# A layer of windowed attention and a gated MLP on one core: first-chunk norm in pairs, smaller first loads of Q and K, and crossbar-DMA transposes

## The chip, the core and the metric

The kernel runs on one core of one Trainium2 chip. The metric is device time in microseconds (us); lower is better. Times below are the median of 13 runs of the kernel before, and the profile is one execution taken with the hardware profiler.

## What is computed

One sequence of S = 2048 rows of width D = 640, in bf16. Both branches read the same normalised input, and everything is added to the residual:

```
xn  = layernorm(x)                                  # over D, no scale or shift
q, k, v = split(xn @ wqkv)                          # 32 heads of 20
scores  = (q @ k.T) * 20**-0.5, kept where 0 <= row - col < 256
attn    = softmax(scores) @ v @ wo
mlp     = (sigmoid(xn @ w_gate) * (xn @ w_up)) @ w_down     # F = 1536
out     = x + attn + mlp
```

## The kernel before

The rows are worked off in four chunks of 512 rows (`NCH`), each of four blocks of 128 rows (`SBC`). Heads go in eight groups of four (`NG`, `HG`): four heads lie in the four 32-row strips of TensorE, so that four small matmuls run side by side.

**Norm and turning.** `ln_block` (L191) takes the statistics of one block on VectorE and the power -1/2 on GpSimd. `norm_block` (L203) writes the normalised block `xn` on VectorE. The projections need it with D on the partitions, so `transpose_block` (L209) turns it with five TensorE transposes of 128 by 128 into PSUM, and ScalarE (chunk 0) or VectorE (chunks 1 to 3) copies it into `xnT`. `xnT` has two buffers (`xtp`), `xn` four.

**Q, K and V.** `proj_block` (L227) makes one of five column blocks of Q or K (five matmuls of 128x512), copies it to `st`, and SyncE's queue writes it to a scratch in DRAM (`sq`, `sk`). `spread` (L244) reads it back with each head in a strip of 32 partitions: `qT` and `kT`. The rows that pad 20 to 32 are zeroed once per scratch by `clear` (L147). `proj_v` (L251) makes V of one block in ten matmuls of 128x320.

**Attention.** A group in a chunk goes in steps of up to 512 columns (`STEPS`, L41: key block, first query block, number of query blocks). A step is one call of `scores` (L388): eight or four matmuls into `ps` (L394), two exponentials on ScalarE into `pT` (L400), and causal and window masks on GpSimd (L405, L409). `pv` (L413) multiplies a group's `pT` by V into `acc` (L420), and `finish_group` (L428) divides and turns the result on VectorE into `oc`. `pT` has four buffers. In chunk 0 there are no earlier keys, so its three steps per group are 384, 256 and 512 columns wide.

**MLP and output.** `g_gu` (L315) makes one of twelve column blocks of gate (L319, tanh at L322) and up (L326), joined on VectorE at L330 into `h`. `down` and `outp` (L342, L352) sum the MLP's second product and the attention's projection in one PSUM tile, add x and write out.

**What sets the order.** The order of instructions on every engine is the order of the program (`manual_schedule`). The scores' steps are the skeleton. Between steps, `Fill` (L443) issues dense TensorE work from a list of generators, in amounts that share what is left evenly over the columns that are left (L540); chunk 0's columns count 0.9. The list (L505 to L519) is gate and up of chunk 0 with norms and transposes of chunk 1 mixed in, Q and K of chunk 1 with the norms of chunk 2, V of chunk 1, one block of gate and up of chunk 1, the output of chunk 0 with the transposes of chunk 2, and so on. Three blocks of gate and up are issued ahead of the first scores (L525).

**SyncE's queue** issues nearly all DMAs, in order; a DMA that must wait for its data holds all later ones. Its order at the start is x of chunk 0 and the weights of V, Q, K, the first half of gate and up (L155), and the two clears; then the writes of `sq` and `sk` as they are made, with the whole of `qT` behind the second write of `sk` (L294), then `kT` of group 0 and of groups 1 to 7 (L298, L299); then `load_rest` (L159): the other half of gate and up, x of chunk 1, two clears, `wd`, four copies of `A_wo` into `wo_i`, four loads of `wo` that wait for those copies, and x of chunk 2. DMAs take turns on eight completion semaphores, so that a DMA also waits for the eighth before it.

The line that decides how much work stands between two steps is

```python
        credit += fill.left() * share(c, width) / weight
        weight -= share(c, width)
        credit = fill.pull(credit)
```

Of the kernel before, what the change touches and what calls it, by code (L numbers as in the profile page):

```python
# [8 lines left out]
P = 128  # L9
# [8 lines left out]
NCH = S // CW  # L18
# [26 lines left out]
)  # L45


def steps_of(c):
    out = []
    for pieces in STEPS:  # L50
        here = [p for p in pieces if c > 0 or p[0] >= 0]
        placed, col = [], 0
        for r, q0, n in here:
            placed.append((r, q0, n, col))
            col += n
        out.append((placed, col))
    return out
# [13 lines left out]
def kernel(  # L71
# [16 lines left out]
    def pool(name, bufs, **kw):  # L88
        return ctx.enter_context(tc.tile_pool(name=name, bufs=bufs, **kw))
# [6 lines left out]
    qp = pool("qp", 2)  # L96
    kp = pool("kp", 3)
    vp = pool("vp", 10)
    hp = pool("hp", 13)
    pp = pool("pp", 4)  # L100
    op = pool("op", 8)
    onp = pool("onp", 3)
    tp = pool("tp", 2)
    np_ = pool("np", 1)
    yp = pool("yp", 2)
# [45 lines left out]
    def load_gu(k):  # L151
        for t, w in ((wg, B_w_gate), (wu, B_w_up)):
            nc.sync.dma_start(out=t[k], in_=w.rearrange("(c p) f -> p c f", p=P)[:, :, k * FS:(k + 1) * FS])

    load_gu(0)  # L155
    clear("q", 0)
    clear("k", 0)

    def load_rest():  # L159
        for k in range(1, F // FS):  # L160
            load_gu(k)
        load_x(1)
        clear("q", 1)
        clear("k", 1)
        nc.sync.dma_start(out=wd, in_=B_w_down.rearrange("(c p) d -> p c d", p=P))
        wo_i = tc.dram_tile([HG, NG * DH, D], BF16, name="wo_i")
        for i in range(HG):
            nc.sync.dma_start(out=wo_i[i].rearrange("(g d) n -> g d n", d=DH),
                              in_=A_wo.rearrange("(g i d) n -> i g d n", i=HG, d=DH)[i])
        for i in range(HG):  # L170
            nc.sync.dma_start(out=wo[32 * i:32 * i + 32, :, :],
                              in_=wo_i[i].rearrange("(m j) n -> j m n", j=32))
        load_x(2)
# [17 lines left out]
    def ln_block(c, s):  # L191
        xs = xc[c][:, s, :]
        stats = lnp.tile([P, 2, nc.vector.BN_STATS_DIM], FP32, name="stats")
        for a in range(2):
            nc.vector.bn_stats(out=stats[:, a, :], in_=xs[:, a * 320:(a + 1) * 320])  # L195
        mv = lnp.tile([P, nc.vector.BN_AGGR_DIM], FP32, name="mv")
        nc.vector.bn_aggr(out=mv, in_=stats)
        rstd = lnp.tile([P, 1], FP32, name="rstd")
        nc.gpsimd.tensor_scalar(out=rstd, in0=mv[:, 1:2], scalar1=EPS, scalar2=None, op0=ADD)
        nc.gpsimd.tensor_tensor(out=rstd, in0=rstd, in1=neghalf, op=POW)  # L200
        return mv, rstd

    def norm_block(c, s, mv, rstd):  # L203
        xn = lnp.tile([P, D], BF16, name="xn", bufs=4)
# [1 line left out]
                                scalar2=rstd[:, 0:1], op0=SUB, op1=MULT)  # L206
        xns[c, s] = xn

    def transpose_block(c, s, act):  # L209
        xn = xns.pop((c, s))  # L210
        pt = ps_d.tile([P, DC, P], BF16, name="pt", tag="d")
        for d in range(DC):
            nc.tensor.transpose(pt[:, d, :], xn[:, d * P:(d + 1) * P], ident)  # L213
        dst = xnT[c][:, :, s * P:(s + 1) * P]
        if act:
            nc.scalar.copy(out=dst, in_=pt)
        else:
            nc.vector.tensor_copy(out=dst, in_=pt)

    def new_xnT(c):  # L220
        xnT[c] = xtp.tile([P, DC, CW], BF16, name="xnT")
# [44 lines left out]

    MM = 216

    def g_norms(c):

        new_xnT(c)
        stat = {}
        for s in range(SBC + 2):
            if s < SBC:
                stat[s] = ln_block(c, s)
                yield 0
            if s >= 2:
                norm_block(c, s - 2, *stat[s - 2])
                yield 0

    def g_transposes(c):
        for s in range(SBC):
            transpose_block(c, s, False)
            yield 5 * 64

    def chain(*gens):
        for g in gens:
            yield from g

    def g_qk(c):  # L290
        for w in "qk":
            for m in range(DC):
                proj_block(w, c, m)
                if w == "k" and m == 1:  # L294
                    spread("q", c, 0, NG)
                yield 5 * MM
        if c == 0:
            spread("k", c, 0, 1)  # L298
            spread("k", c, 1, NG)  # L299

    def g_v(c):
        for s in range(SBC):
# [82 lines left out]
            yield from outp(c, s, ys)  # L385


    def scores(c, g, placed, width):  # L388
        pt = pp.tile([P, HG, CW], BF16, name="pT")
        pss = [ps_s.tile([P, 2, CW], FP32, name="ps", tag="s") for _ in range(2)]  # L390
        for r, q0, n, col in placed:
            kc, kb = divmod(c * SBC + r, SBC)
            for i in range(HG):
                nc.tensor.matmul(  # L394
                    pss[i // 2][:, i % 2, col * P:(col + n) * P],
                    lhsT=qk["k", kc][32 * i:32 * i + DH, g, kb * P:(kb + 1) * P],
                    rhs=qk["q", c][32 * i:32 * i + DH, g, q0 * P:(q0 + n) * P],
                    start=True, stop=True)
        for a in range(2):
            nc.scalar.activation(out=pt[:, 2 * a:2 * a + 2, 0:width * P],  # L400
                                 in_=pss[a][:, :, 0:width * P], func=EXP, scale=SCALE)
        for r, q0, n, col in placed:
            if r >= 0:
                v = pt[:, :, col * P:(col + 1) * P]
                nc.gpsimd.affine_select(out=v, in_=v, pattern=[[0, HG], [1, P]], compare_op=GE,  # L405
                                        fill=0.0, base=0, channel_multiplier=-1)
            if q0 + n - 1 == r + 2:
                v = pt[:, :, (col + n - 1) * P:(col + n) * P]
                nc.gpsimd.affine_select(out=v, in_=v, pattern=[[0, HG], [-1, P]], compare_op=GE,  # L409
                                        fill=0.0, base=-1, channel_multiplier=1)  # L410
        return pt

    def pv(c, g, parts):  # L413
        acc = ps_a.tile([P, CW], FP32, name="acc")
        flat = [(pt, *piece) for placed, pt in parts for piece in placed]
        for k, (pt, r, q0, n, col) in enumerate(flat):
            v = vt[c * SBC + r]
            for i in range(HG):
                h = g * HG + i
                nc.tensor.matmul(  # L420
                    acc[32 * i:32 * i + 32, q0 * P:(q0 + n) * P],
                    lhsT=v[:, h * VW:h * VW + 32], rhs=pt[:, i, col * P:(col + n) * P],
                    start=(k == 0), stop=(k == len(flat) - 1), skip_group_check=True)
        finish_group(c, g, acc)
# [57 lines left out]
            yield cost  # L482

    new_xnT(0)
    stat = {0: ln_block(0, 0)}
    for s in range(SBC + 1):
        if s + 1 < SBC:
            stat[s + 1] = ln_block(0, s + 1)
        if s < SBC:
            norm_block(0, s, *stat[s])  # L490
            transpose_block(0, s, True)
        if s:
            proj_v(0, s - 1)
    for _ in g_qk(0):
        pass
    load_rest()
# [4 lines left out]
    def later(c):  # L501
        load_x(c)
        yield 0

    fill.add("gu0", mix(g_gu(0, 0, 12), chain(g_norms(1), g_transposes(1)), 9), 12 * GU + 1280)  # L505
    fill.add("qk1", mix(g_qk(1), g_norms(2), 2), 50 * MM)
    fill.add("v1", g_v(1), 40 * 136)
    fill.add("gu1a", g_gu(1, 0, 1), 1 * GU)
    fill.add("out0", mix(g_out(0), g_transposes(2), 1, 3), OUT + 1280)
    fill.add("x3", later(3), 0)  # L510
    fill.add("qk2", g_qk(2), 50 * MM)
    fill.add("v2", g_v(2), 40 * 136)
    fill.add("gu1b", mix(g_gu(1, 1, 12), g_norms(3), 10), 11 * GU)
    fill.add("out1", mix(g_out(1), g_transposes(3), 1, 3), OUT + 1280)
    fill.add("qk3", g_qk(3), 50 * MM)
    fill.add("v3", g_v(3), 40 * 136)
    fill.add("gu2", g_gu(2, 0, 12), 12 * GU)
    fill.add("out2", g_out(2), OUT)
    fill.add("gu3", g_gu(3, 0, 12), 12 * GU)  # L519

    todo = [(c, g, k, placed, width) for c in range(NCH) for g in range(NG)
            for k, (placed, width) in enumerate(steps_of(c))]
    share = lambda c, w: w * (0.9 if c == 0 else 1.0)
    weight = sum(share(c, w) for c, *_, w in todo)
    fill.pull(6 * 5 * MM)  # L525
    parts = {}
    credit = 0
    fill.shut = {"out0", "out1", "out2"}
    for t, (c, g, k, placed, width) in enumerate(todo):
        if g == 0 and k == 0 and c > 0:  # L530
            fill.until(f"qk{c}")
        if g == 0 and k == 2 and c > 0:
            fill.until(f"v{c}")
        if k == 1 and t > 3:
            before = todo[t - 3][0:2]
            pv(*before, parts.pop(before))
            if before[1] == NG - 1:
                fill.shut.discard(f"out{before[0]}")
        parts.setdefault((c, g), []).append((placed, scores(c, g, placed, width)))
        credit += fill.left() * share(c, width) / weight  # L540
        weight -= share(c, width)
        credit = fill.pull(credit)
    fill.pull(10 ** 9)

# [47 lines left out]
```

## Time and profile before

| | |
|---|---|
| median of 13 runs | 335.68 us (334.32 to 339.35) |
| the profiled execution: its own time, its span | 339.18 us, 337.5 us |
| TensorE busy (share of the span) | 319.7 us (95%) |
| ScalarE, GpSimd, VectorE busy | 218.4, 165.4, 163.4 us |
| mean granted TensorE clock | 0.99 |
| moved by DMA | 30.89 MB, mean 92 GB/s |

The profiled execution lies near the upper end of the 13 runs, 3.5 us above their median. Its time is 1.7 us more than its span. In the views, times are microseconds from the span's start. A row of the timeline gives start, length, engine, line, operation, tiles, count, and in brackets the idle time of the engine before it with what ended it. A row of the waits gives the total, the number and the longest. Matmuls are pipelined, so the distance between the starts of two rows tells more of what a matmul costs than its length: five matmuls of 128x512 start 1.08 us before whatever follows them. The row of 40 slices cuts the span into pieces of 8.4 us.

### The profile page before, as it was taken

Reading aid. Unit: us, or ns where it says so; the run is one execution under the profiler, and the core shown is the slowest. Engines: PE = TensorE matmul, PEld = TensorE weight load, DVE = VectorE, ACT = ScalarE, POOL = GpSimd, SP = SyncE. Lnnn points to the kernel's source line nnn. Section 1 sums busy time; section 2 is a strip of 40 time slices with the busy share of each in tenths; the row PEclk is TensorE's granted clock in tenths of the full one; section 3 lists DMA queues with packets and bytes.
Section 4 is the critical chain, followed back from the end, with each engine's and each line's share of the span. In section 5 each row is a group of like instructions: output and inputs, shape, how many; then the busy total and the mean of one; then the engine's idle time right before and its main releaser. Section 6 shows DMA issues by size and latency. Waiting matters only on the chain.

```text
span 337.5 us, 7190 instructions
## 1 busy us (share of the span) xinstructions
PE 319.7 (95%) x2855; PEld 166.3 (49%) x2884; DVE 163.4 (48%) x333; ACT 218.4 (65%) x274; POOL 165.4 (49%) x312
## 2 busy tenths in 40 slices
PE   5999878998999999999999999999999999999996
PEld 2654323444556654544445664544445665444664
DVE  4241239678763344655873436354443424444142
ACT  2424674877775667787875666878787666888300
POOL 5200239468665554664865555545555455554300
PEclk9699999999999999999999999999999999999999
DMA  7937798402720024530000002540000010000001
GB/s 260 378 121 217 252 383 286 119 33 82 213 81 22 19 64 163 175 126 0 3 2 19 21 21 94 183 150 2 2 0 3 21 40 20 2 0 2 0 13 66
DMA packets 26224, 30.89 MB, mean 92 GB/s; under 512 B 1456, under 2 KB 25648, under 8 KB 26160
## 3 DMA queue, kind: packets, MB, share of 16 engines
q1 hardware_dynamic: 25904, 30.20, 27.3%
q8 instruction: 22, 0.36, 0.4%
q10 hardware_dynamic: 288, 0.25, 0.2%
q14 instruction: 10, 0.08, 0.1%
HBM read 21.00 MB, written 10.26 MB: 93 GB/s over the span
## 4 chain that ended last, share of the span: by engine, by line
PE 82%; DMA 7%; ACT 4%; DVE 3%; issue 2%; POOL 1%; SPq 1%; POOLq 0%; ACTq 0%
PE y L345 15%; PE pqk L234 13%; PE pg L319 12%; PE pu L326 12%; PE ps L394 8%; PE pv L260 7%; PE y L358 7%; PE acc L420 6%; DMA xc<-in_A_x_dram 5%; ACT pT L400 3%; PE pt L213 1%; DMA sk<-st 1%; DVE stats L195 1%; POOL pT L405 1%; DVE t L430 0%
## 5 line engine op out<-in xcount | busy, mean ns | idle before, releaser
L400 ACT ACTIVATE pT<-ps 128x1024 bf16<-128x1024 f32 (+2 forms) x192 | 175.9, 971 | 61.8 <-PE ps L394 58.0
L405 POOL TENSOR_SCALAR_AFFINE_SELECT pT<-pT 128x512 bf16<-128x512 bf16 x128 | 82.1, 641 | 82.5 <-ACT pT L400 82.3
L409 POOL TENSOR_SCALAR_AFFINE_SELECT pT<-pT 128x512 bf16<-128x512 bf16 x112 | 72.1, 644 | 57.9 <-ACT pT L400 57.9
L330 DVE SCALAR_TENSOR_TENSOR h<-th,pu 128x512 bf16<-128x512 f32 x48 | 32.8, 682 | 60.0 <-PE pu L326 21.4
L319 PE MATMUL pg<-xnT,wg 128*128 128x512 bf16 x229 | 59.2, 380 | 2.6 <-DVE h L330 2.0
L326 PE MATMUL pu<-xnT,wu 128*128 128x512 bf16 x230 | 57.8, 380 | 1.2 <-issue 1.1
L345 PE MATMUL y<-wd,h 128*128 128x320 bf16 x384 | 57.3, 300 | 0.0
L234 PE MATMUL pqk<-xnT,wqkv 128*128 128x512 bf16 x192 | 45.8, 381 | 0.5 <-issue 0.2
L394 PE MATMUL ps<-qT,kT 20*128 20x384 bf16 (+2 forms) x704 | 39.6, 275 | 5.4 <-ACT pT L400 4.0
L345 PEld LDWEIGHTS <-h 128*128 128x128 bf16 x384 | 35.7, 98 | 16.8 <-issue 4.0
L322 ACT ACTIVATE th<-pg 128x512 f32<-128x512 f32 x48 | 28.8, 600 | 14.9 <-PE pg L319 14.8
L430 DVE STREAM_TRANSPOSE t<-acc 128x512 f32<-128x512 f32 x32 | 22.8, 713 | 28.5 <-PE acc L420 28.1
L319 PEld LDWEIGHTS <-wg 128*128 128x128 bf16 x240 | 22.1, 98 | 29.2 <-issue 5.5
L326 PEld LDWEIGHTS <-wu 128*128 128x128 bf16 x240 | 21.3, 98 | 27.0 <-issue 5.2
L234 PEld LDWEIGHTS <-wqkv 128*128 128x128 bf16 x200 | 22.3, 119 | 19.3 <-issue 2.9
L363 DVE SCALAR_TENSOR_TENSOR y_sb<-y,xc 128x320 bf16<-128x320 f32 x32 | 15.4, 490 | 32.6 <-PE y L358 32.6
L394 PEld LDWEIGHTS <-kT 20*128 20x128 bf16 x704 | 12.3, 92 | 37.0 <-issue 35.3
L260 PE MATMUL pv<-wqkv,xnT 128*128 128x320 bf16 x160 | 26.4, 319 | 0.3 <-DVE v L264 0.3
L420 PE MATMUL acc<-pT,v 128*32 128x384 bf16 (+2 forms) x704 | 25.7, 277 | 0.5 <-POOL pT L405 0.2
L358 PE MATMUL y<-wo,oc 128*128 128x320 bf16 x160 | 24.1, 299 | 0.0
L420 PEld LDWEIGHTS <-v 128*32 128x32 bf16 x704 | 15.0, 96 | 13.6 <-issue 11.0
L238 DVE CAST st<-pqk 128x512 bf16<-128x512 f32 x20 | 13.7, 687 | 15.4 <-PE pqk L234 13.7
(32 smaller groups left out, 176.8 us busy)
## 6 DMA issues: line engine op xcount, KB each, us to landing
qT<-sq SPq DMA_DIRECT2D x4, 1024.0 KB, 6.1
kT<-sk SPq DMA_DIRECT2D x3, 1024.0 KB, 5.5
sq<-st SPq DMA_DIRECT2D x20, 128.0 KB, 2.1
sk<-st SPq DMA_DIRECT2D x20, 128.0 KB, 3.3
wqkv<-in_A_wqkv_dram SPq DMA_DIRECT2D x3, 800.0 KB, 6.6
out_dram<-y_sb SPq DMA_DIRECT2D x15, 160.0 KB, 1.8
wg<-in_B_w_gate_dram SPq DMA_DIRECT2D x2, 960.0 KB
wu<-in_B_w_up_dram SPq DMA_DIRECT2D x2, 960.0 KB
```

The costliest lines, as they stand in the source:

```text
L234: nc.tensor.matmul(ps, lhsT=wt[:, m, :], rhs=xnT[c][:, d, :], start=(d == 0), stop=(d == DC - 1))
L260: nc.tensor.matmul(ps[:, 0:HALF], lhsT=xnT[c][:, d, s * P:(s + 1) * P], rhs=wqkv[:, d, 2 * D + hf * HALF:2 * D + (hf + 1) * HALF], start=( ...
L319: nc.tensor.matmul(pg, lhsT=part(wg, d, f), rhs=xnT[c][:, d, :], start=(d == 0), stop=(d == DC - 1))
L326: nc.tensor.matmul(pu, lhsT=part(wu, d, f), rhs=xnT[c][:, d, :], start=(d == 0), stop=(d == DC - 1))
L330: nc.vector.scalar_tensor_tensor(out=h, in0=th, scalar=1.0, in1=pu, op0=ADD, op1=MULT)
L345: nc.tensor.matmul(ys[hf], lhsT=ht[c, f][:, s * P:(s + 1) * P], rhs=wd[:, f, hf * HALF:(hf + 1) * HALF], start=(f == 0), stop=False)
L358: nc.tensor.matmul(ys[hf], lhsT=oc[c, m][:, s * P:(s + 1) * P], rhs=wo[:, m, hf * HALF:(hf + 1) * HALF], start=False, stop=(m == DC - 1))
L394: nc.tensor.matmul(pss[i // 2][:, i % 2, col * P:(col + n) * P], lhsT=qk["k", kc][32 * i:32 * i + DH, g, kb * P:(kb + 1) * P], rhs=qk["q", ...
L400: nc.scalar.activation(out=pt[:, 2 * a:2 * a + 2, 0:width * P], in_=pss[a][:, :, 0:width * P], func=EXP, scale=SCALE)
L405: nc.gpsimd.affine_select(out=v, in_=v, pattern=[[0, HG], [1, P]], compare_op=GE, fill=0.0, base=0, channel_multiplier=-1)
L409: nc.gpsimd.affine_select(out=v, in_=v, pattern=[[0, HG], [-1, P]], compare_op=GE, fill=0.0, base=-1, channel_multiplier=1)
L420: nc.tensor.matmul(acc[32 * i:32 * i + 32, q0 * P:(q0 + n) * P], lhsT=v[:, h * VW:h * VW + 32], rhs=pt[:, i, col * P:(col + n) * P], start ...
```

## The change

In words:

1. **Start.** The four blocks of chunk 0 are normed and turned in two pairs: statistics of two blocks, norm and transpose of both, then V of both. Before, each block's statistics came one block ahead of its norm, and V one block behind.
2. **First scores.** `qT` of groups 0 and 1 is loaded behind the second write of `sk`, then `kT` of group 0, `kT` of groups 1 and 2, the rest of `qT` and the rest of `kT`. x of chunk 1 is loaded ahead of the first clears instead of in `load_rest`.
3. **Steps of chunk 0.** Two groups share five steps of 512, 384, 512, 512 and 384 columns, where each group had three steps; 20 steps in place of 24. A group's `pv` comes ahead of the second step after its last one. Chunk 0's columns count fully in the sharing of fill.
4. **Turning.** For chunks 1 to 3 a DMA on SyncE's queue with `transpose=True` goes from `xn` to `xnT` in place of five TensorE transposes and a VectorE copy, 12 blocks in all. For chunks 1 and 2 each is issued soon behind its norm; for chunk 3, whose buffer is then still read, within the output of chunk 1. In chunks 1 to 3 the GpSimd half of the norm is issued one block later.
5. **Buffers and fill.** `h` 13 to 15, `oc` 8 to 7, `on` 3 to 2 buffers; three blocks of gate and up of chunk 1 ahead of the output of chunk 0 in place of one.

The diff, cut:

```diff
+STEPS0 = (
+    ((0, 0, 0, 3), (0, 3, 3, 1)),
+    ((0, 1, 1, 3),),
+    ((0, 2, 2, 2), (1, 2, 2, 2)),
+    ((1, 0, 0, 3), (1, 3, 3, 1)),
+    ((1, 1, 1, 3),),
+)
...
-    hp = pool("hp", 13)
+    hp = pool("hp", 15)
...
-    op = pool("op", 8)
-    onp = pool("onp", 3)
+    op = pool("op", 7)
+    onp = pool("onp", 2)
...
     load_gu(0)
+    load_x(1)
     clear("q", 0)
     clear("k", 0)
...
-        load_x(1)
...
+    def rstd_block(mv):
         rstd = lnp.tile([P, 1], FP32, name="rstd")
...
+    def turn_block(c, s):
+        nc.sync.dma_start(out=xnT[c][:, :, s * P:(s + 1) * P], in_=xns.pop((c, s)), transpose=True)
...
-    def g_norms(c):
+    def g_norms(c, turn):
...
+        mv, rstd = {}, {}
+        for k in range(SBC + 3):
+            if k < SBC:
+                mv[k] = ln_block(c, k)
+            if 0 <= k - 1 < SBC:
+                rstd[k - 1] = rstd_block(mv[k - 1])
+            if k < SBC:
                 yield 0
+            if 0 <= k - 2 < SBC:
+                norm_block(c, k - 2, mv[k - 2], rstd[k - 2])
                 yield 0
+            if turn and 0 <= k - 3 < SBC:
+                turn_block(c, k - 3)
+
+    def g_turns(c):
         for s in range(SBC):
-            transpose_block(c, s, False)
-            yield 5 * 64
+            turn_block(c, s)
+            yield 0
...
                 if w == "k" and m == 1:
-                    spread("q", c, 0, NG)
+                    spread("q", c, 0, NG if c else 2)
...
             spread("k", c, 0, 1)
-            spread("k", c, 1, NG)
+            spread("k", c, 1, 3)
+            spread("q", c, 2, NG)
+            spread("k", c, 3, NG)
...
-    stat = {0: ln_block(0, 0)}
-    for s in range(SBC + 1):
-        if s + 1 < SBC:
-            stat[s + 1] = ln_block(0, s + 1)
-        if s < SBC:
-            norm_block(0, s, *stat[s])
-            transpose_block(0, s, True)
-        if s:
-            proj_v(0, s - 1)
+    for s0 in range(0, SBC, 2):
+        mv = [ln_block(0, s) for s in (s0, s0 + 1)]
+        for s in (s0, s0 + 1):
+            norm_block(0, s, mv[s - s0], rstd_block(mv[s - s0]))
+            transpose_block(0, s)
+        for s in (s0, s0 + 1):
+            proj_v(0, s)
...
-    fill.add("gu0", mix(g_gu(0, 0, 12), chain(g_norms(1), g_transposes(1)), 9), 12 * GU + 1280)
-    fill.add("qk1", mix(g_qk(1), g_norms(2), 2), 50 * MM)
+    fill.add("gu0", mix(g_gu(0, 0, 12), g_norms(1, True), 9), 12 * GU)
+    fill.add("qk1", mix(g_qk(1), g_norms(2, True), 2), 50 * MM)
     fill.add("v1", g_v(1), 40 * 136)
-    fill.add("gu1a", g_gu(1, 0, 1), 1 * GU)
-    fill.add("out0", mix(g_out(0), g_transposes(2), 1, 3), OUT + 1280)
+    fill.add("gu1a", g_gu(1, 0, 3), 3 * GU)
+    fill.add("out0", g_out(0), OUT)
...
-    fill.add("gu1b", mix(g_gu(1, 1, 12), g_norms(3), 10), 11 * GU)
-    fill.add("out1", mix(g_out(1), g_transposes(3), 1, 3), OUT + 1280)
+    fill.add("gu1b", mix(g_gu(1, 3, 12), g_norms(3, False), 8), 9 * GU)
+    fill.add("out1", mix(g_out(1), g_turns(3), 1, 3), OUT)
...
-        if k == 1 and t > 3:
-            before = todo[t - 3][0:2]
-            pv(*before, parts.pop(before))
-            if before[1] == NG - 1:
-                fill.shut.discard(f"out{before[0]}")
+        for group in [x for x in ends if ends[x] == t - 2]:
+            pv(*group, parts.pop(group))
+            if group[1] == NG - 1:
+                fill.shut.discard(f"out{group[0]}")
...
-        credit += fill.left() * share(c, width) / weight
-        weight -= share(c, width)
+        credit += fill.left() * width / weight
+        weight -= width
```

In the changed program SyncE's queue holds the four turning DMAs of chunk 1 behind `load_rest`, that is behind the loads of `wo` and of x of chunk 2; those of chunk 2 stand among the last writes of `sk` of chunk 1, three of the four directly ahead of the load of that chunk's `kT`. Ten steps of scores and three `pv` come ahead of the first matmul of Q of chunk 1.

## The prediction on record

> **What bounds the kernel now.** I read the page first, then the chain of work that ended last, then the timeline of TensorE and of SyncE's queue in the first 75 us.
>
> ```profile
> PE 319.7 (95%) x2855; PEld 166.3 (49%) x2884; DVE 163.4 (48%) x333; ACT 218.4 (65%) x274; POOL 165.4 (49%) x312
> PE   5999878998999999999999999999999999999996
> ACT  2424674877775667787875666878787666888300
> PEclk9699999999999999999999999999999999999999
> DMA  7937798402720024530000002540000010000001
> PE 82%; DMA 7%; ACT 4%; DVE 3%; issue 2%; POOL 1%; SPq 1%; POOLq 0%; ACTq 0%
> ```
>
> TensorE is the bound: from the eleventh slice on (84 us) it is never under 0.9, so there only removed TensorE work can help. Before that, the slices with 8 and 7 hold waits, and the DMA row is high in the fifth to seventh (34 to 59 us: 7, 9, 8). In the chain, 7% is DMA.
>
> ```profile
> 36.57 0.34 PE L394 MATMUL ps<-qT,kT 20*128 20x384 bf16 x4 [0.98 <-DMA kT<-sk]
> ...
> 50.94 1.24 PE L319 MATMUL pg<-xnT,wg 128*128 128x512 bf16 x5 [1.32 <-DVE h L330]
> ...
> 54.33 1.24 PE L319 MATMUL pg<-xnT,wg 128*128 128x512 bf16 x5 [0.69 <-DVE h L330]
> ...
> 58.65 0.45 PE L213 MATMUL pt<-ident,xn 128*128 128x128 bf16 x5
> 58.94 1.24 PE L319 MATMUL pg<-xnT,wg 128*128 128x512 bf16 x5
> ```
>
> The first scores wait 0.98 us for `kT`. The two waits on VectorE have one root: VectorE's statistics of chunk 1 stand ahead of `h` and wait for x, 9.0 us in all:
>
> ```profile
> DVE stats L195 <- DMA xc<-in_A_x_dram: 9.0, 3, 5.3
> ```
>
> The last two timeline rows price a turning: five transposes start 0.29 us before what follows. SyncE's queue shows why x is late, and what a DMA put behind `load_rest` will meet:
>
> ```profile
> 27.28 0.41 SPq L249 DMA_DIRECT2D qT<-sq  x1
> 27.74 2.55 SPq L242 DMA_DIRECT2D sk<-st  x3
> 34.44 0.82 SPq L249 DMA_DIRECT2D kT<-sk  x2
> ...
> 36.47 1.65 SPq L118 DMA_DIRECT2D xc<-in_A_x_dram  x1
> ...
> 55.22 3.53 SPq L171 DMA_DIRECT2D wo<-wo_i  x4
> 58.80 0.65 SPq L118 DMA_DIRECT2D xc<-in_A_x_dram  x1
> ```
>
> The last `sk` writes share the DMA engines with 1 MB of `qT`; x of chunk 1, asked for at 36.47, lands 11.7 us later; the `wo` loads hold the queue until 58.75.
>
> **What the Trainium skill says.** "TensorE: Matmul & The Clock Gate", Part 1: the clock is granted by windows of 3.4 us, half speed after an idle one, full after a busy one. The trace agrees: the granted clock is 0.53 of full in 8 to 10 us and 0.76 in 14 to 16 (stage table), and ten V matmuls take 2.6 us there against 1.36 later. "DMA: Bandwidth & Descriptors", HWDGE ordering: each DMA engine consumes one queue's descriptors in order; it fits x landing late behind 3 MB. For the crossbar there are two prices far apart, and no row of before shows one. "Latency and other measured facts" of the same page: 261 GB/s. "VectorE: DVE Perf Modes", The three transpose paths: 1309 ns for 128x128.
>
> **The change, part by part,** against the profiled execution (339.2 us, span 337.5).
>
> *Start, -1.8.* Before, the second transpose waits for `xn` behind statistics of block 2, whose x landed at 7.51; V starts at 9.52. In pairs, `xn` of block 1 needs only `rstd` (GpSimd done at 7.06), so both transposes are out by 7.8, and the copy of block 0 by 7.6. V of two blocks starts at 7.8, half clock from 8.06. One full window later (11.5) the clock can be full: 13.5 of the 20 matmuls at 0.267 us, the rest at 0.136, end at 12.4; turning of blocks 2 and 3 with ScalarE's copy behind the V copies, to 13.7; 20 V matmuls, to 16.4. Q starts at 16.4 in place of 18.2. Bounds: -0.5 (no window gained) to -3.5 (never half).
>
> *First loads, -1.0.* With 256 KB of `qT` in place of 1 MB, the last `sk` write should land in 2.1 us (the median of `sq` writes) and not in 4.6. It is issued at 28.0, `kT` of group 0 at 30.4, 4.0 earlier than 34.44; landed at 32.4. Three blocks of gate and up end at 16.4 + 10.8 + 6.5 = 33.7, so `kT` is covered by them by 1.3 us and the 0.98 wait goes. Scores start at 33.7 (before 36.57).
>
> *x of chunk 1 early, -2.0* (1.32 + 0.69; bounds 0 and -2.4, from the distances of starts). Its 640 KB go to the end of the first DMA stretch, which is quiet from 18 us on, and delay the clears by 1.8 us; the first `sq` write comes about then. I cost that at nothing: 10 us of Q and K work cover it.
>
> *Transposes off TensorE, -3.4.* 12 blocks x 0.285. All stand in stretches where TensorE is full, or on its way to the next `xnT`. VectorE's 12 copies (0.49 each) go too, worth nothing by themselves.
>
> *Steps of chunk 0, -0.9.* Scores advance 0.33 (512 columns), 0.28 (384), 0.22 (256): eight groups x 0.83 = 6.6, four pairs x 1.55 = 6.2, so -0.4. A change between scores and dense work costs about 0.13 (ten Q matmuls start 2.29 before the next scores, 71.59 to 73.88, for 10 x 0.216); four fewer, -0.5.
>
> *Waits on exponentials in chunk 0, -1.5* (0 to -4). Idle rows <- ACT between 44 and 98 us sum to about 3.3. A step had 1.57 us of fill against 1.63 of exponentials (39.0 / 24) plus 0.44 of tanh; now 2.01 against 1.88 plus 0.56, so TensorE leads by more. I take under half.
>
> Sum: -10.6.
>
> *Second half of gate and up, +0.3* (0 to 1). It is due for the seventh block at about 42 to 43 us; 2.8 MB from 30.4 at the 370 GB/s of this stretch land at 39 to 43.
>
> *The turning DMAs of chunk 1, +3.0* (0 to 26). This is the new wait. Nothing is queued for TensorE but Q of chunk 1, which needs all four blocks. Need: 33.7 + ten scores (3.1) + three `pv` (1.8) + nine blocks (19.4) + changes (1.3) + waits left (1.3) = 60.6. Offer: the queue from `kT` on carries as many bytes as before (7.2 against 7.1 MB, x removed, Q and K split), so it shifts by the 4.0 us of `kT`: x of chunk 2 is issued at 54.8, and since DMA falls quiet at 63.4 before, landed near 59.5. The turning is behind it. 164 KB at 261 GB/s are 0.63 us; the other price gives 5 x 1.309 = 6.5. I take 0.75 per block and 1 us to land, near the first, as five turnings in one DMA share its start: 59.5 + 3 + 1 = 63.5, 2.9 late. SyncE's time to issue them (unknown, 0.4 as a plain DMA to 2) hides behind x if under 1.5.
>
> *Half clock after that wait, +0.6* (0 to 1.7): a 3 us gap may fill most of a window.
>
> *Chunks 2 and 3, 0.* Turning of chunk 2 is due after the output of chunk 0, some 30 us later; chunk 3's after that of chunk 1. Chunk 2's DMAs do stand ahead of `kT` of chunk 1, which before was issued at 89.99 and landed 0.3 us ahead of its scores; the extra work ahead of those scores (two more blocks of gate and up, 4.3 us) is the cover, and is gone if a block costs over 1.5. Buffers of `h`, `oc`, `on`: no wait is moved, as by the fill list's costs the output of a chunk ends some three steps before they are due.
>
> Net -10.6 + 3.9 = -6.7: 332.5 for an execution like the profiled one. That one lies 3.5 above the median of the 13 runs; part of the spread may be the half clock at the start, of which there is then less to gain, so I take -6.2 from the median: **329.5**.
>
> **Rivals.**
> *No wait for the turning.* If x of chunk 2 lands sooner or TensorE is later at Q of chunk 1: -10.3, so 325.9. For it: before, TensorE took 33.5 us from the first scores to Q of chunk 1 for some 28.7 of work counted the same way; a loss like that would cover it. Against: the queue's order.
> *Covers worth less.* Exponential waits stay, the start gains 0.5, x early 1.0, the turning waits 4: 333.5. For it: chunk 0's ScalarE row has 7s and 8s.
> *Slower: a slow crossbar.* At 6.5 us a block the turning of chunk 1 lands at 86.5: 26 us of wait and 1.7 of half clock, against -10.3: 353. It decides from about 2 us a block (4 x 2.05 + 1 + 59.5 is 8 us late, with the half clock all of the gain), and `kT` of chunk 1 adds to it. For it: the price of 1309 ns; before moved no data through the crossbar.
>
> **How the numbers follow.** Likeliest 0.45 (329.5, own range 326.5 to 332.5); no wait 0.23; covers worth less 0.15; slow crossbar 0.17. The low end takes in a start gain of 3.5; the high end, part of the slow crossbar: 323 to 340, leaving out some 4% below and 14% above. This kernel's measurement can tell about 0.5% (1.7 us) from no change. Faster: 0.45 + 0.23 + half of 0.15 = 0.75; same 0.08; slower 0.17.
>
> **What would show it.** Start: Q at 16.4. First loads: `kT` issued near 30.4, no wait before the first scores near 33.7. x: no VectorE wait for x of chunk 1. Turning: TensorE idle about 3 us ahead of the first Q of chunk 1, near 60 to 64, ended by a DMA; blocks landing 0.6 to 1 us apart. After chunk 0 no new idle. The forecast is wrong if the turning lands 2 us apart or more, if SyncE takes over 1.5 us to issue one, or if the queue reaches the turning at another time than 55.

## The result and the profile after

The changed kernel takes 331.99 us (median of 11 runs, 331.78 to 333.17); the kernel before, over the 48 runs that now lie beside it, takes 335.4 (334.19 to 339.35). The ratio is 0.9892, 95% interval 0.9863 to 0.992. The profiled execution of after took 331.86 us with a span of 330.1; that of before took 339.18 with 337.5. So the profiles differ by 7.4 us of span and the medians by only 3.4. That gap is the first thing to explain.

The rows of the page of after that answer to those of before (one digit is 8.25 us):

```profile
PE 313.8 (95%) x2795; PEld 161.0 (49%) x2824; DVE 159.7 (48%) x321; ACT 216.8 (66%) x266; POOL 166.0 (50%) x312
...
PE   6999979798999999999999999999999999999996
...
PEclk9999999999999999999999999999999999999999
DMA  7976999319700123640013113620000000000001
...
PE 75%; ACT 6%; DMA 6%; POOL 4%; DVE 4%; issue 2%; SPq 2%; ACTq 0%
```

TensorE is busy 5.9 us less (part of it is the half clock of before, which counts as busy; either trace lacks 29 matmul records), and its clock has no 6 in the second slice any more. But there are three slices below 9 in the middle (7, 7, 8 at 41, 58 and 74 us), and the chain still has 6% of DMA. TensorE's timeline names the three (brackets: idle time before the row, and what ended it):

```profile
14.68 10.96 PE L250 MATMUL pqk<-xnT,wqkv 128*128 128x512 bf16 x49
...
32.04 0.40 PE L414 MATMUL ps<-qT,kT 20*128 20x384 bf16 x8
...
43.05 0.68 PE L440 MATMUL acc<-pT,v 128*32 128x384 bf16 x16
44.95 0.34 PE L414 MATMUL ps<-qT,kT 20*128 20x384 bf16 x2 [1.23 <-ACT pT L420]
45.87 0.34 PE L414 MATMUL ps<-qT,kT 20*128 20x384 bf16 x2 [0.58 <-ACT pT L420]
...
62.94 1.25 PE L250 MATMUL pqk<-xnT,wqkv 128*128 128x512 bf16 x4 [1.32 <-DMA xnT<-xn]
...
81.68 0.84 PE L276 MATMUL pv<-wqkv,xnT 128*128 128x320 bf16 x5 [1.21 <-DVE v L280]
```

Q of chunk 0 starts at 14.68 (before 18.17), the first scores at 32.04 without a wait (before 36.57 with one of 0.98), Q of chunk 1 at 62.94 (before 70.04). The wait at 62.94 is the forecast one, at 1.32 us in place of 2.9. The waits at 44.95, 45.87 and 81.68 were not forecast. ScalarE's timeline shows what is behind the first two:

```profile
43.88 1.94 ACT L420 ACTIVATE pT<-ps 128x1024 bf16<-128x1024 f32 x2 [3.24 <-DMA sk<-pT]
```

and VectorE's what is behind the third:

```profile
80.40 0.83 DVE L222 TENSOR_SCALAR xn<-xc,mv,rstd 128x640 bf16<-128x640 bf16 x1 [1.38 <-POOL rstd L217]
81.15 1.90 DVE L280 CAST v<-pv 128x320 bf16<-128x320 f32 x4
```

The exponentials at 43.88 are ended by a DMA that has nothing to do with scores: `sk<-pT` is a clear. The zeros for the clears lie in a buffer of the pool of `pT`, and that pool has four. The fourth step is the first to come round to it, and must wait until the last clear has read it. In the kernel before, the trace has ScalarE's own wait for the clears only at 52.3 us, ahead of the seventh step (52.71), when they had landed. The second fence is VectorE: `xn` waits for GpSimd's `rstd`, and V's copies, which TensorE needs, are queued behind it.

SyncE's queue in after (start and length of the issuing) shows why neither the clears nor the turning came sooner:

```profile
28.42 0.82 SPq L265 DMA_DIRECT2D kT<-sk  x2
...
32.67 1.69 SPq L163 DMA_DIRECT2D sq<-pT  x1
34.40 0.60 SPq L163 DMA_DIRECT2D sk<-pT  x1
...
49.82 3.29 SPq L185 DMA_DIRECT2D wo<-wo_i  x4
53.15 0.43 SPq L132 DMA_DIRECT2D xc<-in_A_x_dram  x1
53.64 5.53 SPq L234 DMA_TRANSPOSE xnT<-xn  x4
```

The last clear is issued at 34.40 and lands at 43.8, behind the other half of gate and up (two loads of 960 KB). The four turnings are issued behind x of chunk 2, as forecast, from 53.64 to 59.17 (forecast: x at 54.8), and the last of them lands at 62.8 (forecast 63.5). TensorE was ready for them at 61.6.

### The profile page after: what moved, and what is told of

The parts are those of the page before. It is cut to its first block, busy times and chain, and to the rows that moved or that the text cites. A ratio compares the mean times of both kernels' runs of the same rounds, so it can differ in the third digit from the quotient of the medians.

```text
span 330.1 us, 7084 instructions
## 1 busy us (share of the span) xinstructions
PE 313.8 (95%) x2795; PEld 161.0 (49%) x2824; DVE 159.7 (48%) x321; ACT 216.8 (66%) x266; POOL 166.0 (50%) x312
## 2 busy tenths in 40 slices
DMA packets 34320, 32.86 MB, mean 100 GB/s; under 512 B 9552, under 2 KB 33744, under 8 KB 34256
## 4 chain that ended last, share of the span: by engine, by line
PE 75%; ACT 6%; DMA 6%; POOL 4%; DVE 4%; issue 2%; SPq 2%; ACTq 0%
PE y L365 13%; PE pg L339 12%; PE pu L346 12%; PE pqk L250 11%; PE ps L414 8%; PE y L378 7%; PE acc L440 6%; PE pv L276 6%; ACT pT L420 5%; DMA sk<-pT 3%; DMA xnT<-xn 1%; POOL pT L425 1%; POOL rstd L217 1%; DVE stats L209 1%; POOL pT L429 1%
## 5 line engine op out<-in xcount | busy, mean ns | idle before, releaser
L420 ACT ACTIVATE pT<-ps 128x1024 bf16<-128x1024 f32 (+1 forms) x184 | 174.9, 1004 | 64.2 <-PE ps L414 60.3
L346 PE MATMUL pu<-xnT,wu 128*128 128x512 bf16 x236 | 58.9, 380 | 0.5 <-issue 0.5
L250 PE MATMUL pqk<-xnT,wqkv 128*128 128x512 bf16 x190 | 45.1, 381 | 2.2 <-DMA xnT<-xn 1.3
L346 PEld LDWEIGHTS <-wu 128*128 128x128 bf16 x240 | 22.2, 98 | 27.9 <-issue 3.3
L339 PEld LDWEIGHTS <-wg 128*128 128x128 bf16 x240 | 21.3, 98 | 27.9 <-issue 6.7
L276 PE MATMUL pv<-wqkv,xnT 128*128 128x320 bf16 x160 | 23.8, 300 | 1.3 <-DVE v L280 1.2
```

The lines of the kernel that those rows point to most:

```text
L250: nc.tensor.matmul(ps, lhsT=wt[:, m, :], rhs=xnT[c][:, d, :], start=(d == 0), stop=(d == DC - 1))
L276: nc.tensor.matmul(ps[:, 0:HALF], lhsT=xnT[c][:, d, s * P:(s + 1) * P], rhs=wqkv[:, d, 2 * D + hf * HALF:2 * D + (hf + 1) * HALF], start=( ...
L339: nc.tensor.matmul(pg, lhsT=part(wg, d, f), rhs=xnT[c][:, d, :], start=(d == 0), stop=(d == DC - 1))
L346: nc.tensor.matmul(pu, lhsT=part(wu, d, f), rhs=xnT[c][:, d, :], start=(d == 0), stop=(d == DC - 1))
```

## The experiments

In all of them the kernel before ran on the same chip: 335.13, 335.09 and 336.19 us (medians) beside the three sets, each on one chip. Its 75 runs there fall into three groups by the mean granted TensorE clock of the run: 45 runs at 0.998 or more with a median of 334.76 (334.25 to 335.68), 26 at about 0.995 with 336.70, and 4 at about 0.99 with 338.94. One stretch of 3.4 us at half clock takes 0.005 from the mean of a run of 335 us, two take 0.01, so the groups are runs with none, one and two such half-clock windows. That is the key to the gap between profiles and medians, as the first experiments show. At full clock the medians of before differ by 0.1 us between the three sets (334.84, 334.73, 334.78), so runs of different sets can be compared.

The theories: either the start's gain in the profile (3.5 us) is real and something in the middle takes it back, or it is only the half clock of that one execution, and the median gains little there. And in the middle: either the wait for the clear and the wait for the turning add up, or each covers the other, so that a fix of one alone gives nothing. The old reasons for each part of the change (transposes, steps, loads, x) are tried last.

### Only the start in pairs, and all but it

Before with the start of after (`start_only`):

```diff
-    stat = {0: ln_block(0, 0)}
-    for s in range(SBC + 1):
-        if s + 1 < SBC:
-            stat[s + 1] = ln_block(0, s + 1)
-        if s < SBC:
+    for s0 in range(0, SBC, 2):
+        stat = {s: ln_block(0, s) for s in (s0, s0 + 1)}
+        for s in (s0, s0 + 1):
             norm_block(0, s, *stat[s])
             transpose_block(0, s, True)
-        if s:
-            proj_v(0, s - 1)
+        for s in (s0, s0 + 1):
+            proj_v(0, s)
```

> The kernel before with the start in pairs alone. Theory A (the half clock of the first 15 us is an accident of some runs of the kernel before, and the pairs only remove it): median within 1.2 us of before (334.2 to 335.4), and the runs above 337 us gone. Theory B (the pairs save the 3.5 us in every run that the two profiled executions show): median 331.9, 1.0% less.

Measured: 335.09 us (334.83 to 335.62, 22 runs), ratio 0.999 [0.9974, 1.0006]. Every one of the 22 runs is at 0.999 or 1.0 of the clock.

After with the start of before (the inverse edit, `after_old_start`):

> The changed kernel with the old start (block by block, V one behind). Theory A: median 332 to 333.2, with some runs near 335.5 like the upper runs of the kernel before. Theory B: median 335.5, every run.

Measured: 332.87 us (331.5 to 335.35, 10 runs), ratio 0.9917 [0.9885, 0.9948]: theory A's 332 to 333.2 with some runs near 335.5, and not theory B's 335.5. Q of chunk 0 in the kernel with the pairs alone:

```profile
14.58 0.59 PE L234 MATMUL pqk<-xnT,wqkv 128*128 128x512 bf16 x2
```

and in after with the old start:

```profile
14.32 1.03 PE L250 MATMUL pqk<-xnT,wqkv 128*128 128x512 bf16 x4
```

The old order reaches Q at 14.32, sooner than the pairs (14.58, and 14.68 in after), when its clock stays full; in the profiled execution of before it was 18.17. The stage table of that execution shows why (stretch; length; busy time of TensorE, its weight loads, VectorE, ScalarE and GpSimd with their counts; TensorE's granted clock; DMA share; GB/s):

```profile
8.00:10.00 2.00, 0.99 (x7) 0.81 (x8) 1.93 (x8) 0.24 (x1) 1.07 (x4) 0.53 1.03 373
10.00:12.00 2.00, 2.00 (x9) 1.14 (x8) 0.95 (x2) 0.88 (x2) 1.37 (x8) 0.50 1.06 371
12.00:14.00 2.00, 2.00 (x12) 1.36 (x11) 0.00 (x0) 1.12 (x2) 0.00 (x0) 0.50 1.06 375
14.00:16.00 2.00, 2.00 (x16) 1.37 (x15) 0.00 (x0) 1.05 (x3) 0.00 (x0) 0.76 1.06 372
```

Half clock for 1.88 + 2 + 2 + 0.96 = 6.8 us (each stretch times twice what is missing to 1), two windows of the 3.4 us that the Trainium skill gives ("TensorE: Matmul & The Clock Gate", Part 1). Only 4 of the 75 runs of before have two. In before, pairs take the half clock away in all runs, cost 0.3 us where there was none (334.76 to 335.09), and leave the median where it was (335.13 to 335.09): theory A. Their worth there is a narrower spread. In the changed kernel they do show in the median, by 0.9 us (332.87 to 331.99), as the old start has more runs above 333; the two ranges overlap, and which windows those runs had was not traced.

### More warm-up in the kernel before

```diff
-        for k in range(6):
+        for k in range(10):
```

(`before_warm`: in the warm-up's two batches, with `stop` moved to the last; 20 matmuls in place of 12).

> The kernel before with 20 warm-up matmuls in place of 12, which fill TensorE's idle time from 5.7 to 7.3 us and change nothing else. Theory A (the upper runs of the kernel before are those in which that idle time brings the half clock): median 334.4 to 335, runs above 336.5 us gone or rare. Rival (their cause is elsewhere): the same spread, 334.2 to 339.

Measured: 335.54 us (334.73 to 338.64, 14 runs), ratio 1.0008 [0.9981, 1.0035]. 13 of 14 runs are at 0.999 or more, against 18 of 28 of before on this chip: the warm-up does keep the clock, but the full-clock runs now spread up to 336.8, so the median gains nothing and misses the 334.4 to 335 of theory A. The profiled execution (335.77, full clock) shows a cost that the expectation left out:

```profile
8.17 0.72 PE L213 MATMUL pt<-ident,xn 128*128 128x128 bf16 x10
9.39 1.53 PE L260 MATMUL pv<-wqkv,xnT 128*128 128x320 bf16 x10 [0.51 <-ACT xnT L216]
...
15.39 4.91 PE L234 MATMUL pqk<-xnT,wqkv 128*128 128x512 bf16 x22
```

The warm-up runs until 8.17 here, and the first transposes, whose `xn` was written at 6.3, stand behind it. Q of chunk 0 starts at 15.39, 1.07 later than with the old start at full clock (14.32), and the run is 1.0 slower than the full-clock median. Whether the other runs spread for the same reason was not traced.

### The two waits before Q of chunk 1

First the zeros in another buffer, so that the exponentials needn't wait for a clear (`zero_h`):

```diff
-    zero = pp.tile([P, HG, CW], BF16, name="pT")
+    zero = hp.tile([P, CW], BF16, name="h")
...
-        nc.sync.dma_start(out=rows.rearrange("h (a e) -> h a e", a=4), in_=zero[:, 0:3, :])
+        nc.sync.dma_start(out=rows.rearrange("h (a b e) -> h a b e", a=4, b=3),
+                          in_=zero[:, None, :].to_broadcast([P, 3, CW]))
```

> The changed kernel with the zeros for the clears taken from an h buffer and not from a pT buffer, so that the fourth step's exponentials don't wait for the second pair of clears. Theory C (that wait is a new one, 3.2 us on ScalarE and about 2 us on TensorE, and ate the gain on exponentials): 330.0, 2 us less than the changed kernel. Rival (TensorE then only waits longer for the turning DMAs of chunk 1, which end at a time that SyncE's queue sets): 331.9, no change, with the wait ahead of the first Q of chunk 1 grown from 1.3 to about 3.4 us.

Measured: 334.04 us (332.26 to 334.64, 11 runs), ratio 0.9945 [0.9922, 0.9968], slower than after. TensorE in it:

```profile
43.49 0.34 PE L415 MATMUL ps<-qT,kT 20*128 20x384 bf16 x4
...
58.81 0.34 PE L415 MATMUL ps<-qT,kT 20*128 20x384 bf16 x4
62.17 2.04 PE L251 MATMUL pqk<-xnT,wqkv 128*128 128x512 bf16 x5 [3.01 <-DMA xnT<-xn]
```

Its stage table:

```profile
60.00:64.00 4.00, 1.83 (x5) 0.58 (x5) 0.49 (x1) 0.76 (x2) 1.23 (x2) 0.81 0.24 49
64.00:68.00 4.00, 4.00 (x35) 1.62 (x34) 1.74 (x3) 1.94 (x2) 1.07 (x2) 0.76 0.10 33
```

The wait at 44 is gone, and the turning's grew from 1.32 to 3.01: Q of chunk 1 starts 0.77 sooner only. That is the rival of the expectation, not theory C; the one run at full clock (332.26) is where the rival put it (331.9). And the gap of 3 us in one piece has a half-clock window behind it (0.19 x 2 x 4 + 0.24 x 2 x 4 = 3.4 us); by their mean clock 10 of 11 runs have at least one such window. The loss of clock stood in none of the expectations; it makes the net a loss.

Then the other wait alone: the loads of `wo` and of x of chunk 2 issued behind the turning of chunk 1 (`wo_late`).

```diff
-        for i in range(HG):
...
-        load_x(2)
...
+    def rest():
+        load_x(2)
+        load_wo()
+        yield 0
+
+    fill.add("rest", rest(), 0)
     fill.add("qk1", mix(g_qk(1), g_norms(2, True), 2), 50 * MM)
```

> The changed kernel with the loads of wo and of x of chunk 2 issued behind the turning DMAs of chunk 1. If the 1.3 us wait ahead of the first Q of chunk 1 is set by what stands ahead of the turning in SyncE's queue: wait gone, 330.7. If the crossbar itself were slow, the wait would stay and the time 332. Rival: x of chunk 2 now comes late and VectorE waits for it in the Q and K of chunk 1: 332 to 334.

Measured: 332.03 us (330.71 to 332.51, 6 runs), ratio 0.9887 [0.9859, 0.9914], as after. The forecast 330.7 is met by one run at full clock (330.71); the other two at full clock took 331.55 and 331.77. Its profiled execution, one of the other three (332.30), has no wait at Q of chunk 1, but a half-clock window behind the waits at 44 to 46, as TensorE's timeline and the stage table show:

```profile
44.87 0.34 PE L419 MATMUL ps<-qT,kT 20*128 20x384 bf16 x2 [1.13 <-ACT pT L425]
45.78 0.34 PE L419 MATMUL ps<-qT,kT 20*128 20x384 bf16 x2 [0.58 <-ACT pT L425]
```

```profile
46.00:50.00 4.00, 4.00 (x20) 1.29 (x18) 3.64 (x8) 2.19 (x4) 3.92 (x8) 0.62 1.56 329
```

Its first Q of chunk 1, in TensorE's timeline:

```profile
62.85 1.27 PE L255 MATMUL pqk<-xnT,wqkv 128*128 128x512 bf16 x5
```

After with the old start has the same window in its profile (0.57 in 46 to 50) and Q of chunk 1 at 63.08, with no wait. So two chains end together at Q of chunk 1. TensorE's, with the wait for the clear, is ready at 61.6 with full clock and about 63 with a half-clock window; the queue's lands the turning at 62.0 (zeros in `h`) to 62.8 (after). Shortening one alone gives at most the distance to the other. This is also why the six runs of after with a clock of 0.995 (332.3 in the median) took hardly longer than the five at 1.0 (332.0), as far as their window lies there (none of the six was traced): it can be swallowed by the turning's wait.

Both edits together (`zero_wo`):

> The changed kernel with both: zeros for the clears in an h buffer, and the loads of wo and of x of chunk 2 behind the turning DMAs of chunk 1. Theory D (each of the two alone only moved the idle time, and what is left of it brings the half clock; together both waits go and no gap of over 1 us is left in chunk 0 for the clock to fall in): 329.0 us or less, clock 1.0 in nearly all runs. Rival (the half clock comes by itself whatever the gaps): 330.5, with 0.995 in half of the runs.

Measured: 328.79 us (328.69 to 329.93, 6 runs), ratio 0.9796 [0.9754, 0.9838], all at full clock.

```profile
43.64 0.34 PE L420 MATMUL ps<-qT,kT 20*128 20x384 bf16 x4
...
58.96 0.34 PE L420 MATMUL ps<-qT,kT 20*128 20x384 bf16 x4
59.24 1.27 PE L256 MATMUL pqk<-xnT,wqkv 128*128 128x512 bf16 x5
```

Q of chunk 1 starts at 59.24, 3.7 sooner than in after, and the kernel is 3.2 faster. Alone the two edits gave +2.1 and 0.0; in runs at full clock +0.3 (one run) and -0.4 (three). So the new waits cost 3.2 us in the middle of the kernel, and each hides the other. Theory D holds, and its rival, a half clock that comes whatever the gaps, does not.

The third wait (V's copy behind `xn`), on top of that, with the norms of chunk 2 starting one unit earlier within Q and K of chunk 1 (`zero_wo_n1`):

```diff
-    fill.add("qk1", mix(g_qk(1), g_norms(2, True), 2), 50 * MM)
+    fill.add("qk1", mix(g_qk(1), g_norms(2, True), 1), 50 * MM)
```

> The same with the norms of chunk 2 one unit earlier in the Q and K of chunk 1, so that the last of them doesn't stand ahead of the V copies on VectorE. If the 1.2 us wait of TensorE for a V copy comes from that norm (which waits for GpSimd behind the masks): 1.2 us less than without. If x of chunk 2, now loaded later, holds VectorE: up to 2 us more.

Measured: 328.03 us (327.92 to 328.48, 6 runs), ratio 0.9768 [0.9723, 0.9812], the fastest of all versions here. The wait of 1.21 is gone; one for the copy of Q takes part of its place, so that 0.76 of 1.21 is gained:

```profile
69.48 1.24 PE L256 MATMUL pqk<-xnT,wqkv 128*128 128x512 bf16 x5 [0.53 <-DVE st L260]
```

### Transposes at the new places, but on TensorE

After with five TensorE transposes and a VectorE copy where the turning DMA stands (`pe_turn`):

```diff
     def turn_block(c, s):
-        nc.sync.dma_start(out=xnT[c][:, :, s * P:(s + 1) * P], in_=xns.pop((c, s)), transpose=True)
+        xn = xns.pop((c, s))
+        pt = ps_d.tile([P, DC, P], BF16, name="pt", tag="d")
+        for d in range(DC):
+            nc.tensor.transpose(pt[:, d, :], xn[:, d * P:(d + 1) * P], ident)
+        nc.vector.tensor_copy(out=xnT[c][:, :, s * P:(s + 1) * P], in_=pt)
```

> The changed kernel with TensorE transposes and VectorE copies in place of the turning DMAs, at the same places. By the prediction's terms (3.4 us of TensorE saved, 1.3 to 1.4 given back in the wait for the turning of chunk 1): 334.0, with no wait ahead of the first Q of chunk 1. Rival (the DMA turning is the whole gain): 335.4. Rival (it gains nothing, as the wait takes it): 332.0.

Measured: 338.43 us (337.03 to 339.91, 15 runs), ratio 1.0074 [1.0046, 1.0103], slower than before, and outside all three expectations (332.0 to 335.4). Right behind the norm, TensorE stands in order behind a transpose whose `xn` isn't there:

```profile
55.68 0.45 PE L237 MATMUL pt<-ident,xn 128*128 128x128 bf16 x5 [1.21 <-DVE xn L222]
...
83.83 0.60 PE L237 MATMUL pt<-ident,xn 128*128 128x128 bf16 x5 [1.68 <-DVE xn L222]
```

and the clock is halved twice: from 46.4 to 49.9 behind the wait for the clear, which is still in this kernel (0.57 in 46 to 50), and from 84.0 to 87.4 behind the wait of 1.68 (0.75 and 0.83 in 82 to 86 and 86 to 90). No run has the full clock: five are at 0.995 (337.4), ten at 0.99 (338.8). In after a DMA in the same place holds no TensorE instruction; only its landing counts. So the place behind the norm suits the DMA and not the transposes.

### One part undone at a time, where the clock stays full

The kernel with both edits of the queue and the zeros (328.79) has no half-clock window, so parts can be priced on it. The transposes on TensorE at the places of before, with their costs in the fill list (`zw_pe`):

> The kernel with both waits removed (zero_wo, 328.8), with TensorE transposes and VectorE copies for chunks 1 to 3 at the places of the kernel before (behind all norms of a chunk; those of chunk 2 in the output of chunk 0). Prediction's term: 12 x 0.285 = 3.4 us more, 332.2, with no half clock. Rival (the large loss of pe_turn is the price of TensorE transposes themselves): 335 or more.

Measured: 332.32 us (331.81 to 334.04, 6 runs), ratio 0.9889 [0.9843, 0.9934]: 3.5 more. The size is the forecast 3.4, but its make-up isn't 12 x 0.285. Of the 3.6 us between the spans of the two profiles some 1.9 is idle time of TensorE: two waits of 2.6 in all that the crossbar version doesn't have and one of 0.69 for a load, against shorter waits elsewhere. From the output of chunk 0 to the end, with eight of the twelve blocks and hardly any waits, it is only 1.1 longer. The two waits:

```profile
53.57 0.44 PE L243 MATMUL pt<-ident,xn 128*128 128x128 bf16 x5 [1.09 <-DVE h L364]
56.62 0.44 PE L243 MATMUL pt<-ident,xn 128*128 128x128 bf16 x5 [1.53 <-DVE xnT L244]
```

The three old steps per group, and chunk 0's share of 0.9 (`zw_steps`):

```diff
-        steps = [[(g + a, *p) for a, *p in st] for g in range(0, NG, 2) for st in STEPS0]
+        steps = [[(g, *p) for p in st if p[0] >= 0] for g in range(NG) for st in STEPS]
...
-        credit += fill.left() * width / weight
-        weight -= width
+        credit += fill.left() * share(c, width) / weight
+        weight -= share(c, width)
```

> zero_wo with chunk 0's three steps per group and its columns counted 0.9, as before. Prediction's terms: 0.9 us more for scores and changes, and 1.5 for exponentials: 331.2. Rival (the wider steps gain only what they save on TensorE): 329.7. Rival (pairs of groups bring waits of their own): 328.5 or less.

Measured, six runs: 327.86, 327.96 and 330.01 at full clock, 331.01 at 0.995, 332.79 and 333.03 at 0.99. Without the two at 0.99 the median is 329.0, 0.2 more than with merged steps; that of the three at full clock, 327.96, is 0.8 less. The profiled one (327.96) has a wait that the version with merged steps doesn't have:

```profile
86.67 0.34 PE L420 MATMUL ps<-qT,kT 20*128 20x384 bf16 x4 [1.26 <-DMA kT<-sk]
```

The fence is TensorE's timeline at the first scores of chunk 1. TensorE's idle time from the first scores on is the same in the two profiles, 4.0 us. So with the full clock the merged steps show no gain, and two of three such runs are faster without them; what they may be worth is fewer runs at half clock. Those three were not traced, and six runs are few: the size of either effect is open.

The whole of `qT` behind the second write of `sk`, and `kT` of groups 1 to 7 in one load (`zw_loads`):

```diff
-                    spread("q", c, 0, NG if c else 2)
+                    spread("q", c, 0, NG)
...
-            spread("k", c, 1, 3)
-            spread("q", c, 2, NG)
-            spread("k", c, 3, NG)
+            spread("k", c, 1, NG)
```

> zero_wo with the whole of qT loaded behind the second write of sk and kT of groups 1 to 7 in one, as before. Prediction's term: 1.0 us more from the wait ahead of the first scores, 329.8. The queue behind shifts by some 3 to 4 us too; if the turning of chunk 1 is late for that, up to 331.

Measured: 329.93 us (329.62 to 331.97, 6 runs), ratio 0.9821 [0.9779, 0.9862]: 1.1 more, and the wait is back where before had it:

```profile
33.28 0.40 PE L418 MATMUL ps<-qT,kT 20*128 20x384 bf16 x8 [1.32 <-DMA kT<-sk]
```

x of chunk 1 in `load_rest`, as before (`zw_x1`):

```diff
     load_gu(0)
-    load_x(1)
     clear("q", 0)
...
             load_gu(k)
+        load_x(1)
         clear("q", 1)
```

> zero_wo with x of chunk 1 loaded behind the second half of gate and up, as before. Prediction's term: 2.0 us more, 330.8. As the norms and so the turning of chunk 1 come later, Q of chunk 1 may wait on top and the half clock come back: up to 334.

Measured: 330.42 us (330.18 to 330.66, 6 runs), ratio 0.9827 [0.9789, 0.9865]: 1.6 more, from the two waits on `h` that before had:

```profile
45.88 1.24 PE L352 MATMUL pu<-xnT,wu 128*128 128x512 bf16 x5 [0.83 <-DVE h L356]
51.62 1.24 PE L345 MATMUL pg<-xnT,wg 128*128 128x512 bf16 x5 [1.03 <-DVE h L356]
```

## Why the prediction came out as it did

The forecast of faster was right and the range held the time; 329.5 was 2.5 us too low. Against the profiled execution it looks better still (332.5 forecast, 331.86 measured), but that is luck, with errors of both signs: the start gained 1.7 more there than forecast and the turning cost 2.3 less with its half clock, while the steps did not gain their 2.4 and two waits came that were not forecast. By its steps:

- **Start, -1.8.** In the profile it was -3.5, as two whole windows went and not one. Between medians it is 0.0, at full clock +0.3. The step that failed is the one at the end, "so I take -6.2 from the median": I saw that the profiled execution was 3.5 above the median and that part might be the half clock, and took off only 0.5. That execution belongs with the 4 of 75 runs that have two windows. The start's gain is the windows' cost, and in the median there is none to gain. That is 1.3 to 1.6 us of the 2.5.
- **First loads, -1.0.** Right: -1.1 on its own. `kT` is issued at 28.42 where 30.4 was forecast (the start moved more than forecast), and the wait is gone.
- **x of chunk 1, -2.0.** Right: -1.6.
- **Transposes, -3.4.** Right as a sum (3.5 with the other version at the old places), but about half of it is waits that go with the transposes, and the work alone is worth about half of 12 x 0.285. That the two make 3.5 is luck.
- **Steps -0.9 and exponentials -1.5.** Wrong: with the full clock, undoing the steps cost nothing (two of three runs were 0.8 faster). The waits for exponentials in chunk 0 are 3.2 us in before and 2.9 in after, 1.8 of these for the clear. They fall to 1.25 with both edits, but with three steps per group they are no longer (1.1). So what shortened them is not the number of steps. In before, too, the zeros hold a buffer of `pT`, until the clears land at 50 us; that this is the reason was not tested.
- **The turning's wait, +3.0.** The mechanism was right, at the forecast instruction and the forecast queue position. In after it is 1.32, because TensorE had lost about 2 us to a wait that I didn't see, the one at 44 to 46. With that one removed it is 3.01, near the 2.9 of the forecast; need and landing then both come 1.4 to 1.5 earlier than forecast. The price of 0.75 us a block was less than issuing alone takes (1.3 in the median), and one issue of chunk 2 took 2.26, over the 1.5 that was named as a sign of being wrong; no TensorE wait of after follows it.
- **The half clock after it, +0.6.** It isn't in the profile of after; with a 3 us gap it is, and a window costs 1.9 us in before's groups (336.70 - 334.76).
- **Not forecast:** the zeros' buffer, and V's copy behind `rstd` (1.21). The prediction said of buffers that "no wait is moved" for `h`, `oc` and `on`; it didn't ask the same of `pT`, where in after the fourth step in place of the seventh meets the zeros. Which part of the change moved that was not tested.

At full clock before takes 334.76 and after 332.0, so -2.8. By the experiments: start +0.3, first loads -1.1, x -1.6, transposes -3.5, steps +0.8 (from the three full-clock runs), and the two waits ahead of Q of chunk 1 +3.2, together -1.9. 0.9 stays open. The parts were undone on the version without those waits and one at a time; the fill order, the earlier clears and the GpSimd half of the norm were not priced alone.

Of the rivals, "covers worth less" was nearest in its reason: the exponential waits stayed and the start gained nothing, but x gave 1.6 and not 1.0, and the turning waited 1.3 and not 4. (Its own terms give 333.8, not 333.5.) "No wait for the turning" (325.9) is refuted for the kernel as it is. The slow crossbar is refuted: in `wo_late` the trace has the first three turnings of chunk 1 landing 0.5 to 0.6 us apart (53.18, 53.77, 54.31), near the 0.63 that the prediction worked out from the 261 GB/s.

## What to carry to other kernels

When a new wait shows up, ask whether a second chain ends at the same instruction: two waits ahead of one consumer can hide each other, so that each fix alone reads as worthless or worse and only both together pay. Before costing a stall from one profiled execution, see whether its granted clock is that of the median run; time lost to a half clock in the profile isn't time that a typical run can gain. A change in the steps or their order can also shift which step meets a buffer that something else still holds, so follow each pool's rotation, the one that a DMA reads from too.

## What the runs showed of the hardware

- The clock is granted by windows of 3.41 us, as the Trainium skill has it ("TensorE: Matmul & The Clock Gate", Part 1), but a window need not be idle as a whole to be followed by half clock. In the stage tables of `zero_h`, `wo_late` and after, cut at the windows of each trace (stretch, length, TensorE busy with its count, granted clock, DMA share, GB/s):

```profile
59.06:62.47 3.41, 0.40 (x6) 1.00 0.86 77
62.47:65.89 3.42, 3.42 (x16) 0.50 0.00 0
...
43.51:46.92 3.41, 1.71 (x16) 1.00 1.07 371
...
41.94:45.35 3.41, 2.12 (x24) 1.00 1.05 384
```

  The window of `wo_late` that ends at 46.92 has half clock behind it, as its line for 46 to 50 above shows. After has nearly the same two waits (1.23 and 0.58 us against 1.13 and 0.58), but its windows are cut elsewhere, no window holds both waits whole, and the clock stays full. Over the 14 traces, every full-clock window in which TensorE was busy for less than 0.43 of the time was followed by half clock (8 windows), none in which it was busy for more than 0.51, and two of the seven between.
- A turning of 128x640 by DMA took 1.2 to 2.3 us of SyncE's time in after (median 1.3). The landing can be told for three of the twelve: 2.6, 4.9 and 6.8 us after the issue. The row of the DMA view of after:

```profile
xnT<-xn SPq DMA_TRANSPOSE x12, 4.9
```

- Packets of under 512 bytes number 9552 in after, 1456 in before and 1488 with the transposes back on TensorE (`pe_turn`). What they cost other DMAs was not measured.
